# Weight sums moved forward by one slot, and three more units by seven products

## The chip, the cores and the metric

The kernel runs on one core of a Trainium2 chip. The metric is the device time of one execution in microseconds (us). The engines that matter here: TensorE (PE) multiplies, VectorE (DVE), ScalarE (ACT) and GpSimd (POOL) work elementwise, and SyncE (SP) issues nearly all DMAs. GpSimd doesn't touch the accumulators of TensorE (PSUM) in this kernel.

## The reference

Eight batches of eight heads. `x` has 512 rows of 64 numbers for each head, `state` has 32 rows. Both attend to each other, and the two readings, 544 rows for each batch, become the rows of a two-layer network with a 512 x 2048 and a 2048 x 512 matrix:

```python
a = softmax(0.125 * x @ state.T);   xread = a @ state
a2 = softmax(0.125 * state @ x.T);  sread = a2 @ x
rows = concatenate([xread, sread])        # per batch 544 rows of 8*64 = 512 numbers
h = rows @ w_in
out = (h * tanh(softplus(h))) @ w_out     # float32
```

## The kernel before

Every float32 product is made of three products of a high and a low part (high x high, high x low, low x high), each a fast matmul. The hidden width of 2048 is cut into 8 **slots** of 256. After a start in which the weights are read and batch 0 is computed, the kernel goes through **rounds** (`key`), one for each batch from 1 on. A round has 8 **lines**, one for each slot j, and the order of all work is written out by hand in `TABLE`: each word is a step, and every engine executes its instructions strictly in the order of the steps (class `InOrder`, which also is why nearly all instructions have line L73, the helper that records them).

The first layer of a line is G0 M0 G1 M1: twelve matmuls of 512 columns into two PSUM banks named `ph` (G0 the first bank, G1 the second), and ScalarE's activation out of each (`u<-ph`, M0 and M1). The pool `ps_h` has these two banks only; N0 at the end of a round, 32 small matmuls `swp` that make the next batch's first-layer weights, takes the same two banks (`first_bank`).

The second layer is done in **units** (batch, p, j): 256 of a batch's rows (p is 0 or 1) and slot j. P and p prepare a unit (`prepare`): high and low parts `gh` and `gl`. A and B consume a unit on TensorE (`consume`). At most three units are ready at once, and units are consumed some lines after they are prepared: the p=0 units of a batch in the last lines of its own round, the p=1 units in the first lines of the next round.

A unit is a 2 x 2 block product. It is done with eight block products, 12 matmuls of 512 columns (`acc_top`, `acc_end`), or in Winograd's way with seven, 21 matmuls of 256 columns into four banks (`acc_one`, `acc_two`, `acc_top`, `acc_end`). `sevens(key, p)` says for how many of a batch's eight slots the seven products are used. Seven need sums of the blocks on both sides: of the unit (`sums`, three GpSimd additions in P, then a ScalarE cast and a VectorE subtraction in p), and of the slot's weights, once for each slot. `seven_weights(j)`, the step T with the slot's number, makes the latter in four pieces, one at each mention of T in the table:

1. VectorE adds the stored high and low weights into `w_sums`; there is one buffer of it, so that this waits until the slot before is through with it.
2. GpSimd makes the four sums (VectorE for slot 7).
3. ScalarE casts them to the high parts: `wo<-w_sums` and `wx<-w_sums`. The first takes the place of a part of the slot's own weights that only eight products need.
4. VectorE subtracts for the low parts (`wo<-w_sums,wo`, `wx<-w_sums,wx`).

Where all eight slots of a (batch, p) use seven products, `merged` joins two of the last product's three matmuls into one of 512 columns, and the finish (`sums_of`, `result`) has one more addition. `sums_of` empties the banks `one` and `two` at the start of the first eight-product unit, or in the last unit.

Steps around the change: TU transposes softmax weights on VectorE (`u<-e`) and issues 16 DMAs that spread them (`e2T<-u`, on SP's queue); li issues the load of the next batch's x (`x_in`) behind them; the results' stores (`out_dram<-o`, `out_dram<-sums`) come behind these on the same queue. PR0 and PR1 transpose (`at<-e`, DVE), cast (`ah<-at`, ACT) and subtract (`al`, DVE) the other softmax; NO normalises it; X0 to X3 transpose `x_in` (DVE). sr0 and sr1 scale the state's readings (`srds`, DVE).

Of the kernel before, what the change touches and what calls it, by code (L numbers as in the profile page):

```python
# [17 lines left out]
P = 128  # L18
B, H, S, NS, D = 8, 8, 512, 32, 64
# [5 lines left out]
SLOTS = NFC // 2  # L25
# [1 line left out]
LAG = 2  # L27
WARM = 5
UNITS = 10
FIRST = 3  # L30
G = 4 * P


def as_f32(ap):
    return ap.bitcast(F32)
# [45 lines left out]
def state_attention_mish_kernel(ctx, tc, x, state, w_in, w_out, out):  # L81

    nc = tc.nc
    pe, dve, act, pool_e = (InOrder(tc, e) for e in (nc.tensor, nc.vector, nc.scalar, nc.gpsimd))
# [809 lines left out]
    S1, S3, S2, S4 = range(3, 7)  # L894
    T3, T4, T2 = range(3)
    wx = {}

    def weight_sums(j, n, m=1):


        q = 3 * j + n
        tag, first, count = ("w_in", 0, 16) if q < 16 else ("sw2", 16, 4) if q < 20 else ("x", 20, 4)
        if tag not in wx:
            wx[tag] = (const if tag == "w_in" else pool).tile([P, count, 2, 256], F32R, tag=tag, name=f"wx_{tag}", bufs=1)
        return wx[tag][:, q - first:q - first + m]

    def seven_weights(j):


        w = pool.tile([P, 4, 256], F32, tag="wt", name=f"w_sums_{j}", bufs=1)  # L910
        dve.tensor_add(
            w.rearrange("p (k e) c -> p k (e c)", k=2), as_f32(wo[j][:, :, 0]), as_f32(wo[j][:, :, 1]))
        yield
        by = dve if j == SLOTS - 1 else pool_e
        by.tensor_sub(w[:, 0], w[:, 0], w[:, 1])
        by.tensor_sub(w[:, 1], w[:, 3], w[:, 1])
        by.tensor_add(w[:, 3], w[:, 3], w[:, 0])
        by.tensor_sub(w[:, 2], w[:, 2], w[:, 3])
        yield
        cut = {5: 1, 6: 2}.get(j, 3)  # L920
        parts = [(w[:, 0], *(wo[j][:, 0, n, 256:] for n in (1, 0)))]
        for a, b in ((0, cut), (cut, 3))[:2 - cut // 3]:
            to = weight_sums(j, a, b - a)
            parts.append((w[:, 1 + a:1 + b], to[:, :, 1], to[:, :, 0]))
        for value, high, _ in parts:
            act.copy(high, value)
        yield
        for value, high, low in parts:
            dve.tensor_sub(low, value, as_f32(high))
# [34 lines left out]
    def prepare():  # L964


        unit = todo.pop(0)
        key, p, j = unit
        u = made.pop(unit).rearrange("f k h t -> f (k h) t")
        hi, lo = (  # L970
            pool.tile([P, W], F32R, tag="g", name=f"{t}_{key}_{p}_{j}", bufs=6).rearrange("f (s t) -> f s t", t=P)
            for t in ("gh", "gl"))
        parts[unit] = hi, lo
        ready.append(unit)
        if j < sevens(key, p):
            sums = pool.tile([P, 4, P], F32, tag="o", name=f"sums_{key}_{p}_{j}", bufs=2)
            pool_e.tensor_add(sums[:, :2], u[:, 1:3], u[:, 3:].to_broadcast([P, 2, P]))
            pool_e.tensor_add(sums[:, 2], sums[:, 0], u[:, 2])
            pool_e.tensor_add(sums[:, 3], sums[:, 2], u[:, 0])
            act.copy(hi[:, :3], u[:, :3])  # L980
            yield
            low_g(u[:, :3], hi[:, :3], lo[:, :3])
            act.copy(hi[:, 3:7], sums)
            low_g(sums, hi[:, 3:7], lo[:, 3:7])
        else:
            act.copy(hi[:, :4], u)
            low_g(u, hi[:, :4], lo[:, :4])
# [10 lines left out]
    def sums_of(key, p, banks):  # L998

        tag, bufs = ("g", 6) if (key, p) in ((1, 1), (B - 3, 1), (B - 2, 0)) else ("wt", 1)  # L1000
        e = banks["sums"] = pool.tile([P, 4, 256], F32, tag=tag, name=f"sums_{key}_{p}", bufs=bufs)
        one, two = (banks[n].rearrange("t (h e) -> t h e", h=2) for n in ("one", "two"))
        act.copy(e[:, 0], one[:, 0])
        dve.tensor_sub(e[:, 3], e[:, 0], one[:, 1])
        dve.tensor_add(e[:, 1:3], two, e[:, 3:].to_broadcast([P, 2, 256]))
        if sevens(key, p) < SLOTS:
            dve.tensor_add(e[:, 3], e[:, 1], two[:, 1])
        else:
            dve.scalar_tensor_tensor(e[:, 3], e[:, 1], -1.0, two[:, 1], ALU.mult, ALU.subtract)
# [63 lines left out]
    def half_slot(key, j, at):  # L1073
# [4 lines left out]
        elif ready and (ready[0][:2] != (key, 0) or ready[0][2] < j + (j == SLOTS - 1 and at)):  # L1078
# [6 lines left out]
            P G0 M0 p G1 M1  # L1085
            P G0 M0 p G1 M1 S4 S6 A S4 S4 S6 S6 T0 T0
            P G0 M0 p G1 M1 sr0 sr1 SC SC A sr0 sr1 SC MM0 MM1 w2 lx TR0 TR1 TR0 TR1
            P G0 M0 p G1 M1 T0 EE0 EE1 EX0 EX1 A T0 P p w3 B NO EE0 EE1 NO T1 T1
            P G0 M0 p G1 M1 A P p TU PR0 PR1 T1 T1 B T2
            P G0 M0 p G1 M1 PR0 PR1 P p PR0 A N0 N2 N0 N0 PR1 li P p B""",  # L1090
        2: """
            P T2 G0 M0 p G1 M1 T2 P T2 p X0 X1 A P X2 X3 p B
            P G0 M0 p G1 M1 P p S2 S2 XD A ST P p B T3
            P T3 G0 M0 p G1 M1 P p w4 A T3 P p T3 B T4
            P T4 G0 M0 p G1 M1 P p A S4 SC T4 S4 S4 SC w5 P p T4 B T5 MM0 MM1
            P G0 M0 p G1 M1 P p TR0 TR1 A P T5 TR0 TR1 p B
            P G0 M0 p G1 M1 S6 sr0 sr1 P p S6 S6 sr0 sr1 T5 EE0 EE1 EX0 EX1 A w2 w3 EE0 EE1 P p T5 B NO
            P G0 M0 p G1 M1 P p NO TU PR0 PR1 A P p B
            P G0 M0 p G1 M1 PR0 PR1 P p PR0 A N0 N2 N0 N0 PR1 li P p B""",
        3: """  # L1100
            P G0 M0 p G1 M1 P p X0 X1 A P X2 X3 T6 p B
            P T6 G0 M0 p G1 M1 P p S2 S2 XD A T6 ST T6 P p B
            P G0 M0 p G1 M1 P p w4 A P p B
            P G0 M0 p G1 M1 P p A S4 SC S4 S4 SC lx w5 P p B MM0 MM1
            P G0 M0 p G1 M1 P p TR0 TR1 A P TR0 TR1 p T7 B T7
            P G0 M0 p G1 M1 S6 sr0 sr1 P p S6 S6 sr0 sr1 EE0 EE1 EX0 EX1 A w2 w3 EE0 EE1 P p B T7 NO
            P G0 M0 p G1 M1 P p T7 NO TU PR0 PR1 A P p B""",
        "steady": """
            P G0 M0 p G1 M1 P p X0 X1 A P X2 X3 p B
            P G0 M0 p G1 M1 P p S2 S2 XD A ST P p B  # L1110
# [32 lines left out]
    for key in [*range(1, B - 1), "s", B - 1]:  # L1143
        if key == "s":
            for i, item in enumerate(items):
                j, r, k = i // 4, i // 2 % 2, i % 2
# [66 lines left out]
        for j, line in enumerate(steps_of(key)):  # L1213
            run = {
                "G": lambda k: first_k(j, k), "M": lambda k: mish_k(j, k),
                "P": lambda _: begin(), "p": lambda _: end(),
                "A": lambda _: half_slot(key, j, 0), "B": lambda _: half_slot(key, j, 1),
                "S": visit_sw,
                "N": next_sw, "T": seven_weights, "w": again, "lx": lambda _: load_natural(), "ly": lambda _: load_last(), "li": lambda _: load_next(),
                "rm": lambda _: moving, "rt": lambda _: sread_transposed(), "W": lambda i: next(items[i]), "U": lambda _: results(), "rs": lambda _: sreads_split(),  # L1220
                "z": at0["sr"], "sr": prev["sr"], "SR": own["sr"], "mm": prev["mm"], "ee": prev["ee"], "tu": prev["tu"],
                "X": own["x"], "XD": own["xd"], "ST": own["st"], "SC": own["sc"], "MM": own["mm"], "EE": own["ee"],
                "TR": own["tr"], "EX": own["ex"], "NO": own["no"], "PR": own["pr"], "TU": own["tu"],
            }
# [37 lines left out]
```

## Time and profile before

| | us |
|---|---|
| median of 3 runs (625.06 to 626.0) | 625.77 |
| the profiled execution | 625.47 |
| its span, first to last instruction | 623.7 |
| PE busy | 616.9 (99%) |
| DVE busy | 447.4 (72%) |
| ACT busy | 367.9 (59%) |
| POOL busy | 233.2 (37%) |

The trace names instructions by what they write and read, `out<-in`. A line of the timeline has the start and the duration in us, the engine, the operation, its tiles, the shape, how many like ones follow each other, and in brackets how long the engine stood idle before and what ended that. A matmul's duration is longer than its share of the stream, since matmuls are pipelined: the pace is read from start to start.

### The profile page before, as it was taken

The numbers are of one execution on the slowest core, as the hardware profiler recorded it, in microseconds if no ns is written. First come the engines' busy times: TensorE is split into PE (matmuls) and PEld (weight loads), VectorE is DVE, ScalarE is ACT, GpSimd is POOL, SyncE is SP. The second block draws the span as 40 slices with busy tenths as digits, with TensorE's granted clock in tenths as the row PEclk, the third lists the DMA queues.
The fourth block names the chain that finished last, engine by engine and source line by source line (L and its number), as shares of the span: only waits on it lengthen the run. The fifth ranks groups of instructions, "written<-read, shape, count | busy, mean of one in ns | idle before, by whom it ended". The sixth has DMA issues, their size and how long they took to land.

```text
span 623.7 us, 13822 instructions
## 1 busy us (share of the span) xinstructions
PE 616.9 (99%) x5388; PEld 534.6 (86%) x5388; DVE 447.4 (72%) x762; ACT 367.9 (59%) x762; POOL 233.2 (37%) x348
## 2 busy tenths in 40 slices
PE   8999999999999999999999999999999999999997
PEld 6777777788888898898988898889889899898997
DVE  5999976666788885969467774869386887535364
ACT  4999876466457454665447555655456766544442
POOL 0000000236366064326632573246522744443284
PEclk9999999999999999999999999999999999999999
DMA  8995922954462164534554265515355332320011
GB/s 318 413 357 149 363 77 68 296 164 125 104 210 69 35 174 117 164 106 132 141 169 136 73 155 164 171 48 163 111 172 166 106 114 91 102 68 25 11 35 35
DMA packets 71969, 88.79 MB, mean 142 GB/s; under 512 B 13792, under 2 KB 49120, under 8 KB 71904
## 3 DMA queue, kind: packets, MB, share of 16 engines
q1 hardware_dynamic: 71472, 87.71, 44.6%
q8 instruction: 43, 0.70, 0.5%
q10 hardware_dynamic: 432, 0.20, 0.1%
q14 instruction: 22, 0.18, 0.1%
HBM read 62.85 MB, written 13.11 MB: 122 GB/s over the span
## 4 chain that ended last, share of the span: by engine, by line
PE 86%; ACT 2%; DVE 1%; DMA 1%; SPq 1%; issue 1%; ACTq 0%; DVEq 0%
PE ph L73 25%; PE acc_top L73 15%; PE acc_one L73 11%; PE acc_two L73 11%; PE acc_end L73 9%; PE swp L73 4%; PE ph_s L73 4%; PE acc L73 2%; PE srp L73 1%; DMA wor<-in_moe_w_out_dram 1%; PE acc_s_one L73 1%; PE acc_s_top L73 1%; PE acc_s_two L73 1%; PE sc L73 1%; ACT wir L73 1%
## 5 line engine op out<-in xcount | busy, mean ns | idle before, releaser
L73 POOL TENSOR_TENSOR sums<-u 128x256 f32<-128x256 f32 x96 | 77.9, 812 | 192.2 <-DVE gl L73 117.0
L73 ACT ACTIVATE u<-ph 128x256 f32<-128x256 f32 x224 | 73.5, 382 | 80.0 <-PE ph L73 78.6
L73 DVE TENSOR_TENSOR gl<-u,gh 128x384 fp32r<-128x384 f32 (+1 forms) x112 | 70.2, 627 | 69.8 <-ACT gh L73 64.5
L73 POOL TENSOR_TENSOR sums<-sums,u 128x128 f32<-128x128 f32 x192 | 113.8, 593 | 15.1
L73 DVE TENSOR_TENSOR gl<-sums,gh 128x512 fp32r<-128x512 f32 x96 | 78.7, 820 | 31.0 <-ACT gh L73 31.0
L73 ACT CAST gh<-u 128x384 fp32r<-128x384 f32 (+1 forms) x112 | 59.2, 529 | 67.4 <-PE acc_end L73 47.7
L73 PE MATMUL acc_top<-wo,gh 128*128 128x256 f32 (+1 forms) x448 | 93.5, 300 | 0.0
L73 POOL TENSOR_TENSOR w_sums<-w_sums 128x256 f32<-128x256 f32 x28 | 25.3, 902 | 152.0 <-ACT gh L73 110.5
L73 ACT CAST gh<-sums 128x512 fp32r<-128x512 f32 x96 | 59.6, 621 | 29.9 <-POOL sums L73 29.8
L73 PEld LDWEIGHTS acc_top<-wo,gh 128*128 128x128 f32 x448 | 71.2, 191 | 4.5 <-issue 1.6
L73 PE MATMUL ph<-ah,swh 128*128 128x512 f32 (+1 forms) x228 | 70.6, 391 | 0.0
L73 PE MATMUL ph<-al,swh 128*128 128x512 f32 (+1 forms) x228 | 69.9, 388 | 0.2 <-DVE al L73 0.2
L73 PE MATMUL ph<-ah,swl 128*128 128x512 f32 (+1 forms) x228 | 69.9, 388 | 0.0
L73 PE MATMUL acc_top<-wo,gl 128*128 128x256 f32 (+1 forms) x224 | 66.9, 299 | 0.0
L73 PEld LDWEIGHTS ph<-al,swh 128*128 128x128 f32 x228 | 42.5, 188 | 10.0 <-DVE al L73 0.4
L73 PEld LDWEIGHTS ph<-ah,swl 128*128 128x128 f32 x228 | 42.6, 188 | 9.3
L73 DVE TENSOR_TENSOR swl<-swp,swh 128x512 fp32r<-128x512 f32 (+1 forms) x60 | 36.3, 645 | 18.6 <-ACT swh L73 18.5
L73 PEld LDWEIGHTS ph<-ah,swh 128*128 128x128 f32 x228 | 39.5, 188 | 8.3 <-issue 0.8
L73 PEld LDWEIGHTS acc_top<-wo,gl 128*128 128x128 f32 x224 | 42.7, 191 | 1.4
L73 PE MATMUL acc<-wo,gh 128*128 128x512 f32 x128 | 40.3, 395 | 0.3 <-DVE wo L73 0.3
L73 ACT CAST swh<-swp 128x512 fp32r<-128x512 f32 (+1 forms) x60 | 30.5, 563 | 16.8 <-PE swp L73 16.8
L73 PE MATMUL acc_one<-wo,gh 128*128 128x256 f32 x192 | 39.8, 289 | 0.0
(233 smaller groups left out, 1393.6 us busy)
## 6 DMA issues: line engine op xcount, KB each, us to landing
w_in<-w_in_again SPq DMA_DIRECT2D x27, 1024.0 KB, 6.1
x<-in_x_dram SPq DMA_DIRECT2D x32, 256.0 KB, 4.4
wir<-in_moe_w_in_dram SPq DMA_DIRECT2D x16, 512.0 KB, 9.4
wor<-in_moe_w_out_dram SPq DMA_DIRECT2D x16, 512.0 KB, 8.9
x_rows<-x_turned SPq DMA_DIRECT2D x56, 128.0 KB, 2.4
out_dram<-sums SPq DMA_DIRECT2D x25, 256.0 KB, 4.4
x_in<-in_x_dram SPq DMA_DIRECT2D x24, 256.0 KB, 4.2
w_in_again<-w_in_sb SPq DMA_DIRECT2D x4, 1024.0 KB, 7.1
```

Of the source, the lines that this page charges most:

```text
L73: made = method(*args, **kwargs)
```

## The change

Slot 1's weight sums (T1) move from the end of line 5 and the line after to stand directly behind slot 0's in line 5 of round 1. Each later slot's steps move up: T3 takes T2's places, T4 takes T3's, and so on, and T2 comes into line 6 of round 1, where T1 ended before, with all four pieces in that line. With sums ready one slot earlier, `FIRST` goes from 3 to 4 and `sevens` gives 7 for (2, 0) and 8 for (2, 1): the units (1, 1, 3), (2, 0, 6) and (2, 1, 7) are made by seven products, and the eight units of (2, 1) by merged ones. Slot 7's four sums move from VectorE to GpSimd.

```diff
--- before.py
+++ after.py
@@ -27,7 +27,7 @@
 LAG = 2
 WARM = 5
 UNITS = 10
-FIRST = 3
+FIRST = 4
 G = 4 * P
 
 
@@ -911,7 +911,7 @@
         dve.tensor_add(
             w.rearrange("p (k e) c -> p k (e c)", k=2), as_f32(wo[j][:, :, 0]), as_f32(wo[j][:, :, 1]))
         yield
-        by = dve if j == SLOTS - 1 else pool_e
+        by = pool_e
         by.tensor_sub(w[:, 0], w[:, 0], w[:, 1])
         by.tensor_sub(w[:, 1], w[:, 3], w[:, 1])
         by.tensor_add(w[:, 3], w[:, 3], w[:, 0])
@@ -950,7 +950,7 @@
         todo += [(key, p, j) for p in range(1 if key == "s" else 2) for j in range(SLOTS)]
 
     def sevens(key, p):
-        return {(1, 0): 0, (1, 1): FIRST, (2, 0): SLOTS - 2, (2, 1): SLOTS - 1}.get((key, p), SLOTS)
+        return {(1, 0): 0, (1, 1): FIRST, (2, 0): SLOTS - 1}.get((key, p), SLOTS)
 
     def merged(key, p):
 
@@ -1085,26 +1085,26 @@
             P G0 M0 p G1 M1
             P G0 M0 p G1 M1 S4 S6 A S4 S4 S6 S6 T0 T0
             P G0 M0 p G1 M1 sr0 sr1 SC SC A sr0 sr1 SC MM0 MM1 w2 lx TR0 TR1 TR0 TR1
-            P G0 M0 p G1 M1 T0 EE0 EE1 EX0 EX1 A T0 P p w3 B NO EE0 EE1 NO T1 T1
-            P G0 M0 p G1 M1 A P p TU PR0 PR1 T1 T1 B T2
+            P G0 M0 p G1 M1 T0 EE0 EE1 EX0 EX1 A T0 T1 T1 P p w3 B NO EE0 EE1 NO
+            P G0 M0 p G1 M1 T1 A T1 P p TU T2 T2 PR0 PR1 T2 T2 B T3
             P G0 M0 p G1 M1 PR0 PR1 P p PR0 A N0 N2 N0 N0 PR1 li P p B""",
         2: """
-            P T2 G0 M0 p G1 M1 T2 P T2 p X0 X1 A P X2 X3 p B
-            P G0 M0 p G1 M1 P p S2 S2 XD A ST P p B T3
-            P T3 G0 M0 p G1 M1 P p w4 A T3 P p T3 B T4
-            P T4 G0 M0 p G1 M1 P p A S4 SC T4 S4 S4 SC w5 P p T4 B T5 MM0 MM1
-            P G0 M0 p G1 M1 P p TR0 TR1 A P T5 TR0 TR1 p B
-            P G0 M0 p G1 M1 S6 sr0 sr1 P p S6 S6 sr0 sr1 T5 EE0 EE1 EX0 EX1 A w2 w3 EE0 EE1 P p T5 B NO
-            P G0 M0 p G1 M1 P p NO TU PR0 PR1 A P p B
+            P T3 G0 M0 p G1 M1 T3 P T3 p X0 X1 A P X2 X3 p B
+            P G0 M0 p G1 M1 P p S2 S2 XD A ST P p B T4
+            P T4 G0 M0 p G1 M1 P p w4 A T4 P p T4 B T5
+            P T5 G0 M0 p G1 M1 P p A S4 SC T5 S4 S4 SC w5 P p T5 B MM0 MM1
+            P G0 M0 p G1 M1 P p TR0 TR1 A P TR0 TR1 p B
+            P G0 M0 p G1 M1 S6 sr0 sr1 P p S6 S6 sr0 sr1 T6 T6 EE0 EE1 EX0 EX1 A w2 w3 EE0 EE1 P p T6 B NO
+            P G0 M0 p G1 M1 T6 P p NO TU PR0 PR1 A P p B
             P G0 M0 p G1 M1 PR0 PR1 P p PR0 A N0 N2 N0 N0 PR1 li P p B""",
         3: """
-            P G0 M0 p G1 M1 P p X0 X1 A P X2 X3 T6 p B
-            P T6 G0 M0 p G1 M1 P p S2 S2 XD A T6 ST T6 P p B
+            P G0 M0 p G1 M1 P p X0 X1 A P X2 X3 T7 p B
+            P T7 G0 M0 p G1 M1 P p S2 S2 XD A T7 ST T7 P p B
             P G0 M0 p G1 M1 P p w4 A P p B
             P G0 M0 p G1 M1 P p A S4 SC S4 S4 SC lx w5 P p B MM0 MM1
-            P G0 M0 p G1 M1 P p TR0 TR1 A P TR0 TR1 p T7 B T7
-            P G0 M0 p G1 M1 S6 sr0 sr1 P p S6 S6 sr0 sr1 EE0 EE1 EX0 EX1 A w2 w3 EE0 EE1 P p B T7 NO
-            P G0 M0 p G1 M1 P p T7 NO TU PR0 PR1 A P p B""",
+            P G0 M0 p G1 M1 P p TR0 TR1 A P TR0 TR1 p B
+            P G0 M0 p G1 M1 S6 sr0 sr1 P p S6 S6 sr0 sr1 EE0 EE1 EX0 EX1 A w2 w3 EE0 EE1 P p B NO
+            P G0 M0 p G1 M1 P p NO TU PR0 PR1 A P p B""",
         "steady": """
             P G0 M0 p G1 M1 P p X0 X1 A P X2 X3 p B
             P G0 M0 p G1 M1 P p S2 S2 XD A ST P p B

```

## Rows read from the trace of the kernel before

**Rows 1.** The page: busy time by engine, its share, instructions.
```profile
PE 616.9 (99%) x5388; PEld 534.6 (86%) x5388; DVE 447.4 (72%) x762; ACT 367.9 (59%) x762; POOL 233.2 (37%) x348
```

**Rows 2.** Waits of PE between 70 and 330 us: total, times, longest.
```profile
PE acc L73 <- DVE wo L73: 0.3, 1, 0.3
```

**Rows 3.** Timeline of PE: starts of (1,1,0), (1,1,1), (1,1,4), (1,1,5).
```profile
148.54 0.40 PE L73 MATMUL acc_one<-wo,gh 128*128 128x256 f32 x2
...
151.05 0.40 PE L73 MATMUL acc_one<-wo,gh 128*128 128x256 f32 x2
...
164.32 0.61 PE L73 MATMUL acc_top<-wo,gh 128*128 128x512 f32 x2
...
167.04 0.61 PE L73 MATMUL acc_top<-wo,gh 128*128 128x512 f32 x2
```

**Rows 4.** Timeline of DVE, lines 5 and 6 of round 1.
```profile
128.52 0.69 DVE L73 TENSOR_TENSOR gl<-u,gh 128x512 fp32r<-128x512 f32 x1 [3.43 <-ACT gh L73]
...
132.79 1.22 DVE L73 TENSOR_TENSOR w_sums<-wo 128x1024 f32<-128x1024 f32 x1
...
134.53 1.30 DVE L73 STREAM_TRANSPOSE u<-e 128x512 f32<-128x512 f32 x2
...
138.82 1.16 DVE L73 TENSOR_TENSOR wx_w_in<-w_sums,wx_w_in 128x768 fp32r<-128x768 f32 x1 [1.50 <-ACT wx_w_in L73]
```

**Rows 5.** Timeline of POOL: T1's four sums.
```profile
134.16 3.76 POOL L73 TENSOR_TENSOR w_sums<-w_sums 128x256 f32<-128x256 f32 x4 [18.67 <-DVE w_sums L73]
```

**Rows 6.** Operations on `w_sums`: count, shortest/median/longest of one in ns.
```profile
L73 POOL TENSOR_TENSOR w_sums<-w_sums x28: 727/924/1294, 111.9 to 230.0; 128x256 f32<-128x256 f32 x28
```

**Rows 7.** Timeline of ACT, lines 6 and 7 of round 1.
```profile
137.95 0.83 ACT L73 CAST wx_w_in<-w_sums 128x768 fp32r<-128x768 f32 x1 [2.30 <-POOL w_sums L73]
138.69 1.20 ACT L73 ACTIVATE u<-ph 128x256 f32<-128x256 f32 x4
...
140.79 0.65 ACT L73 CAST gh<-u 128x512 fp32r<-128x512 f32 x1
```

**Rows 8.** Timeline of PE, end of round 1.
```profile
141.03 1.96 PE L73 MATMUL swp<-w_in,bd 64*32 64x256 f32 x64
```

**Rows 9.** Timeline of DVE, line 5 of round 2 to line 0 of round 3.
```profile
196.20 0.46 DVE L73 TENSOR_SCALAR srds<-srp,rs 128x64 f32<-128x64 f32 x2
...
199.53 0.69 DVE L73 TENSOR_TENSOR gl<-sums,gh 128x512 fp32r<-128x512 f32 x1
200.14 0.42 DVE L73 TENSOR_TENSOR wo<-w_sums,wo 128x256 fp32r<-128x256 f32 x1
...
202.22 0.67 DVE L73 TENSOR_REDUCE s<-e 128x16 f32<-128x512 f32 x1
...
205.99 1.30 DVE L73 STREAM_TRANSPOSE u<-e 128x512 f32<-128x512 f32 x2
...
225.47 1.22 DVE L73 TENSOR_TENSOR w_sums<-wo 128x1024 f32<-128x1024 f32 x1 [0.75 <-DMA out_dram<-sums]
...
227.08 1.23 DVE L73 TENSOR_TENSOR gl<-sums,gh 128x512 fp32r<-128x512 f32 x1
```

**Rows 10.** Timeline of POOL: one unit's three sums.
```profile
195.90 0.75 POOL L73 TENSOR_TENSOR sums<-u 128x256 f32<-128x256 f32 x1
196.73 1.01 POOL L73 TENSOR_TENSOR sums<-sums,u 128x128 f32<-128x128 f32 x2
```

**Rows 11.** Timeline of SP's DMA queue, from line 7 of round 2.
```profile
207.36 10.09 SPq L403 DMA_DIRECT2D e2T<-u  x16
...
219.71 1.39 SPq L693 DMA_DIRECT2D out_dram<-sums  x2
```

**Rows 12.** Timeline of PE: unit (2,1,3), first matmul with its sums' low part.
```profile
229.60 0.28 PE L73 MATMUL acc_one<-wx_w_in,gl 128*128 128x256 f32 x1
```

**Rows 13.** Timeline of PE in the first microseconds.
```profile
1.36 2.50 PE L73 MATMUL warm<-ident 128*128 128x128 f32 x10 [1.36 <-POOL ident masks.py:199]
...
6.13 1.07 PE L73 MATMUL st<-ident,sn 128*64 128x128 f32 x8
```

## The prediction

> **What bounds the kernel now.** I read the page first: TensorE is busy for 616.9 of 623.7 us, no other engine for more than 72% [rows 1]. A matmul's duration holds pipelining, so 99% alone doesn't say that the stream is dense; the waits do. Between 70 and 330 us, the stretch in which every edit lies, TensorE waited once, 0.3 us, for the weights of batch 0 [rows 2]. From then on nothing that the other engines do is late for it. So two things count: how many columns the stream loses, and whether an edit uses up the slack of something that TensorE now finds ready. Gains on VectorE, ScalarE or GpSimd are worth nothing, and no stall is there to remove.
>
> **What the seven products save.** An eight-product unit takes 167.04 - 164.32 = 2.72 us from start to start, a seven-product unit 151.05 - 148.54 = 2.51 [rows 3]: 0.21 each, 0.63 for three. The paces are 2.72/12 = 0.227 us for 512 columns and 2.51/21 = 0.120 for 256, so a merged last product takes 0.227 + 0.120 = 0.347 in place of 0.359: 0.012 for each of the eight units of (2,1), 0.1 in all. Together **-0.7 us**. This is all that the change can bring. Its price off TensorE, for each of the three units: three sums on GpSimd, another cast and another subtraction; for the merged finish one addition. In rounds 4 and on every unit pays this without a wait of TensorE, so I cost them at nothing where no weight sums are made beside them. Slot 7's sums on GpSimd take VectorE out of work at a place where nothing waits: nothing.
>
> **The move of T1 and T2 in round 1.** T1's addition now lies in a hole: VectorE idled 3.43 us before 128.52 [rows 4], and GpSimd had nothing. Free. At 132.79, where it stood, T1's two subtractions come instead (0.42 [rows 9] and 0.96 to 1.16 [rows 4]); that is an exchange of 1.2 against some 1.3, and TU starts at about 134.6 instead of 134.53. T2's addition must wait for the one buffer of `w_sums`, and stands behind TU, whose two transposes take 1.3: it starts at 135.85 and ends at 137.1. GpSimd begins 0.15 after the end of an addition (T1: 134.01, then 134.16 [rows 5]), so T2's sums begin at 137.2. T1's took 3.76 [rows 5]; the 28 sums have 0.727, 0.924 and 1.294 as their least, median and longest [rows 6], so four take 2.9 to 5.2. T2's run beside two transposes and one subtraction only; I take 3.5, near the median, and they end at 140.75.
>
> The Trainium skill, in "SBUF — State Buffer", section "Who interferes with whom", says that VectorE and GpSimd share one pair of ports, that only a VectorE instruction with two inputs in SBUF (or in a two-port mode) contends with GpSimd's reads, and that the second one then blocks for the whole instruction. By that, transposes would cost T2's sums nothing; they would take about 3.1, the stall below would be 1.3, and the sum 0.4 lower. T1's four were of 0.74 to 1.06 us with both kinds beside them, which doesn't decide it.
>
> Now what is queued behind. T2's large cast (`wx<-w_sums`) stands in line 6 and waits for all four sums. ScalarE executes in order, so the four activations of line 7 (M0, M1) stand behind it, and the casts of PR0, PR1 and of unit (1,0,7). In the kernel before this very thing happens with T1: the cast waited 2.30 us for GpSimd and began at 137.95, and the activations ended at 138.69 + 1.20 = 139.89 [rows 7]. That was in time, because N0, which needs both `ph` banks emptied by them, came at 141.03 [rows 8]. With the cast at 140.78 instead of 137.95 all this is 2.8 late: the activations end at 142.7, and N0, with the two banks of the pool taken, starts at 142.75: TensorE stands for **1.7 us**. The cast of (1,0,7), ending at 141.44 before [rows 7], ends at 144.3; N0's 1.9 us last until 144.65, so it is no second wait; its low part, behind T3's addition on VectorE, may be late by 0.1. I take **+1.8**; the ends are 1.1 (sums of 2.9) and 3.4 (sums of 5.2). Nothing later gives this back, as TensorE has no idle time to fill. T3's steps stand where T2's stood, and its weights are needed one unit later; unit (1,1,3)'s new subtractions have a few tenths to spare. T4 and T5 take places of T3 and T4. I count nothing for these.
>
> **The move of T6 into line 5 of round 2.** Times here are those of the kernel before; all of them shift with the first stall. T5's addition of 1.2 us has left the end of line 3, so that VectorE, busy without a break from there, ends `srds` not at 196.66 [rows 9] but at about 195.1 (0.3 of it an estimate for subtractions with no GpSimd beside them). T6's addition follows, until 196.3, and its four sums on GpSimd until 199.95. But the three sums of unit (2,0,5) are now behind them on GpSimd, 1.84 us [rows 10], until 201.8; then the cast, 0.62, and the subtraction `gl<-sums`, which began at 199.53 [rows 9], begins at 202.4 and ends at 203.1. NO's second part, at 202.22 before, with T5's subtractions (2.08 us, 200.14 to 202.22 [rows 9]) ahead of it, starts 0.85 late although these are gone. In line 6 T6's subtractions (1.4, as GpSimd is idle then; 2.08 at most) and the second subtraction of (2,0,6), 0.6, stand ahead of TU, which was at 205.99 [rows 9]: TU is 2.85 late.
>
> TU is the head of a chain on SP's queue: 16 issues of 10.09 us, the load of x, the store of (2,0) at 219.71 [rows 11]. The slot's addition in line 0 of round 3 waits for that store (225.47, idle 0.75 [rows 9]), since `sums` of (2,0) and `w_sums` are one buffer; behind it on VectorE stands `gl<-sums` of unit (2,1,3), which ended at 227.08 + 1.23 = 228.31 [rows 9]. TensorE wanted it at 229.60 [rows 12]: a slack of 1.29. The chain has none before that, so 2.85 late leaves a stall of **1.55**. Its ends: nothing, if TU is less than 1.3 late (T6's sums quick, VectorE ahead), and 3.2, if T6's sums take 5.2.
>
> **The sum.** -0.7 + 1.8 + 1.5 = +2.6 us. The profiled execution of 625.47 (a span of 623.7 and 1.77 around it) becomes 628.1; it lies 0.3 under the median of the runs, so the forecast for the median is 628.4.
>
> **The rivals.**
>
> *No stall, the other side.* GpSimd's sums of T2 are done before ScalarE is needed, and TensorE finds all its banks empty: 625.77 - 0.7 = 625.1. It decides at N0: the large cast must begin before 141.03 - 1.97 = 139.05 (1.97 from its start to the end of the activations [rows 7]), so T2's addition 1.7 us earlier than I place it, or all four sums in 1.8 us. For it: in the kernel before TensorE waited for nothing here, so much slack is about. Against: the buffer of `w_sums` and the order of VectorE, which put the addition behind TU; and no sum was shorter than 0.727 [rows 6].
>
> *The first stall alone.* VectorE keeps more of its lead in lines 4 and 5 of round 2, or the chain on SP is shorter, and the 1.29 us hold: 625.77 - 0.7 + 1.8 = 626.9. For it: the second stall is a difference of long chains. Against: three things of 0.6 to 1.4 us come in ahead of TU.
>
> *The delay piles up.* T6's sums are slow, and unit (2,0,5) and the activations of line 6, behind its cast on ScalarE, are late for TensorE too, another 1.5: 629.9. For it: GpSimd's spread of 0.727 to 1.294.
>
> *The clock falls.* In the first microseconds the 128-column matmuls went at 0.25 us each (2.50 for ten), from 6.13 on at 0.134 [rows 13]: half rate for up to 4.8 us, a loss of 2.4. If a stall of 1.8 us brought that back, once, the time would be 630.8. The Trainium skill ("TensorE: Matmul & The Clock Gate", "HAM oscillation — how this bites in real kernels") says that TensorE's clock falls to half after idling for long enough in one piece. No row here has so long a gap after the start, which leaves it open; the granted clock of the trace is at full speed, 2.4 GHz.
>
> **How the numbers follow.** Forecast 0.45, its own range 627.4 to 629.4 (sums between 2.9 and 4.3 us); first stall alone 0.22; no stall 0.20; pile-up 0.08; clock 0.05. What a measurement can tell from no change is about 0.2%, 1.25 us: 624.5 to 627.0. No case reaches under 624.5 by its rows; I leave 0.04 for a gain that I don't see. Within lie the rest of "no stall" and over half of "first stall alone", 0.16 + 0.14 = 0.30; slower is 0.66. The range of 625.0 to 630.3 goes from the whole saving without a stall to the pile-up.
>
> **What would show it.** In the profile after: T2's four sums on GpSimd right behind TU, beginning near 137.2; ScalarE waiting for them until 140.5 or later; a wait of TensorE for ScalarE's `u` ahead of `swp` at the end of round 1, 1 to 2.5 us; `e2T<-u` of round 2 issued over 1.3 us later than TensorE's own shift; a wait of TensorE for VectorE's `gl` in unit (2,1,3). The chain that ended last would then pass through GpSimd in these two places. The units (1,1,3), (2,0,6) and (2,1,7) would take 2.51 us each from start to start. The prediction is wrong if `swp` follows unit (1,0,6) at once, and wrong in its second part if TU isn't late or if VectorE has the low part of (2,1,3) before TensorE asks for it.

## The result, and the profile after

The changed kernel takes 631.5 us (median of 5 runs, 630.81 to 632.71); beside it the kernel before took 625.51 (624.87 to 626.0). The ratio is 1.010, interval 1.0089 to 1.0111: 6 us slower, and above the range of 625.0 to 630.3. The profiled execution took 631.46, its span is 629.7 (before: 623.7).

The page answers [rows 1]: TensorE is busy 1.9 us longer over a span that is 6.0 longer.

```profile
PE 618.8 (98%) x5407; PEld 535.8 (85%) x5407; DVE 449.0 (71%) x762; ACT 369.8 (59%) x765; POOL 240.3 (38%) x361
```

TensorE's waits between 70 and 330 us answer [rows 2] (total, times, longest):

```profile
PE acc_one L73 <- DVE gl L73: 2.5, 2, 2.1
PE swp L73 <- ACT u L73: 1.1, 1, 1.1
PE acc_top L73 <- ACT gh L73: 0.2, 1, 0.2
```

The first two are the two forecast stalls, at the forecast places. To see what each cost, I set TensorE's starts of the same matmuls in the two traces side by side. The changed kernel was 0.45 ahead at 136 us; 0.42 of that was there at 115 us, before its first moved instruction (T1's addition, 124.85). Such an offset of the start lies between -1.1 and +2.0 us in the traces below. From 136 us on it loses:

| stretch, time of before | lost | what |
|---|---|---|
| 136 to 154 | +2.29 | first stall |
| 154 to 170 | -0.23 | (1,1,3) by seven |
| 170 to 224 | +0.33 | (2,0,6) by seven, -0.21; (2,0,7) late, +0.54 |
| 224 to 232 | +4.27 | second stall, unit (2,1,3) |
| 232 to 250 | -0.22 | (2,1,7) by seven, merged products |
| sum | +6.44 | |

Behind 250 the two run in step to the end; 6.44 less the 0.45 of the start is the 6.0 by which the span grew.

**The saving came.** Timeline of TensorE, unit (1,1,3) and the next product, against [rows 3]:

```profile
160.67 0.40 PE L73 MATMUL acc_one<-wo,gh 128*128 128x256 f32 x2
...
163.19 0.40 PE L73 MATMUL ph<-ah,swh 128*128 128x512 f32 x1
```

2.52 us from start to start; 2.72 by eight products. The three units and the merged products gave 0.23 + 0.21 + 0.22 = 0.66.

**The first stall.** Timelines of GpSimd, ScalarE and TensorE at the end of round 1:

```profile
137.08 3.25 POOL L73 TENSOR_TENSOR w_sums<-w_sums 128x256 f32<-128x256 f32 x4 [7.34 <-DVE w_sums L73]
```
```profile
140.36 0.83 ACT L73 CAST wx_w_in<-w_sums 128x768 fp32r<-128x768 f32 x1 [2.11 <-POOL w_sums L73]
141.10 1.20 ACT L73 ACTIVATE u<-ph 128x256 f32<-128x256 f32 x4
```
```profile
141.81 2.50 PE L73 MATMUL swp<-w_in,bd 64*32 64x256 f32 x64 [1.15 <-ACT u L73]
```

T2's sums are made in 3.25 us; the large cast waits for them, the four activations stand behind the cast, and `swp` begins when the first bank is free and then takes 2.50 in place of 1.96 [rows 8] because the second is emptied last (it is 64 matmuls in both traces, not the 32 named above). So 1.2 is lost ahead of `swp`, 0.5 in it, and 0.5 by the units behind it.

**The second stall.** First SP's queue and VectorE, against [rows 9, 11]:

```profile
212.45 10.61 SPq L403 DMA_DIRECT2D e2T<-u  x16
223.16 2.06 SPq L136 DMA_DIRECT2D x_in<-in_x_dram  x4
225.32 0.92 SPq L693 DMA_DIRECT2D out_dram<-sums  x2
```
```profile
226.04 1.38 DVE L73 STREAM_TRANSPOSE x_turned<-x_in 128x512 f32<-128x512 f32 x2 [1.72 <-DMA x_in<-in_x_dram]
229.45 1.46 DVE L73 STREAM_TRANSPOSE x_turned<-x_in 128x512 f32<-128x512 f32 x2 [2.03 <-DMA x_in<-in_x_dram]
231.66 1.23 DVE L73 TENSOR_TENSOR w_sums<-wo 128x1024 f32<-128x1024 f32 x1 [0.75 <-DMA out_dram<-sums]
232.80 0.55 DVE L73 TENSOR_TENSOR gl<-u,gh 128x384 fp32r<-128x384 f32 x1
233.27 1.22 DVE L73 TENSOR_TENSOR gl<-sums,gh 128x512 fp32r<-128x512 f32 x1
```

Then TensorE, against [rows 12]:

```profile
230.95 0.40 PE L73 MATMUL acc_one<-wo,gh 128*128 128x256 f32 x2
233.40 0.39 PE L73 MATMUL acc_one<-wo,gl 128*128 128x256 f32 x1 [2.05 <-DVE gl L73]
...
234.54 0.58 PE L73 MATMUL acc_one<-wx_w_in,gl 128*128 128x256 f32 x1 [0.46 <-DVE gl L73]
...
237.73 0.63 PE L73 MATMUL ph<-ah,swh 128*128 128x512 f32 x2
```

Shifted by the 1.94 of delay that TensorE had by then, `acc_one<-wx_w_in,gl` was due at 229.60 + 1.94 = 231.54 and came at 234.54: 3.00 late. From it to the end of the unit 3.19 us passed, against 231.52 - 229.60 = 1.92 before: 1.27 more, in which TensorE waits for nothing. That is the clock. Windows of 1 us (the column after those of the five engines is the granted clock):

```profile
233.00:234.00 1.00, 0.60 (x3) 0.42 (x3) 1.00 (x2) 0.03 (x1) 0.94 (x1) 0.91 0.85 206
234.00:235.00 1.00, 0.54 (x3) 0.46 (x3) 1.00 (x2) 0.38 (x1) 0.98 (x1) 0.50 0.83 201
235.00:236.00 1.00, 1.00 (x7) 1.00 (x7) 1.00 (x2) 0.00 (x0) 0.92 (x2) 0.50 0.86 207
236.00:237.00 1.00, 1.00 (x6) 1.00 (x6) 1.00 (x2) 0.00 (x0) 0.92 (x2) 0.50 0.81 198
237.00:238.00 1.00, 1.00 (x8) 0.91 (x7) 1.00 (x3) 0.75 (x2) 0.93 (x2) 0.88 0.45 101
```

At 233.8, 0.4 us behind the first wait and ahead of the second, the clock went to 0.50, which is 1.2 GHz, through three whole windows and parts of two more. The mean clock of the run is 0.997, and it is 0.996 or 0.997 in all five runs of this kernel.

### The profile page after: what moved, and what is told of

Read it like the earlier page. It is cut to its first block, busy times and chain, and to the rows that moved or that the text cites. A ratio compares the mean times of both kernels' runs of the same rounds, so it can differ in the third digit from the quotient of the medians.

```text
span 629.7 us, 13880 instructions
## 1 busy us (share of the span) xinstructions
PE 618.8 (98%) x5407; PEld 535.8 (85%) x5407; DVE 449.0 (71%) x762; ACT 369.8 (59%) x765; POOL 240.3 (38%) x361
## 4 chain that ended last, share of the span: by engine, by line
PE 70%; DVE 7%; SPq 5%; DMA 3%; ACT 3%; issue 2%; POOL 2%; DVEq 0%; ACTq 0%; POOLq 0%
PE ph L73 19%; PE acc_top L73 11%; PE acc_one L73 11%; PE acc_two L73 10%; PE acc_end L73 6%; PE ph_s L73 4%; PE swp L73 4%; SPq L403 3%; DVE gl L73 2%; DMA w_in_again<-w_in_sb 1%; PE acc L73 1%; PE srp L73 1%; POOL w_sums L73 1%; PE acc_s_one L73 1%; PE acc_s_top L73 1%
## 5 line engine op out<-in xcount | busy, mean ns | idle before, releaser
L73 POOL TENSOR_TENSOR sums<-u 128x256 f32<-128x256 f32 x99 | 80.6, 814 | 186.6 <-DVE gl L73 114.6
L73 POOL TENSOR_TENSOR sums<-sums,u 128x128 f32<-128x128 f32 x198 | 116.4, 588 | 15.5
L73 DVE TENSOR_TENSOR gl<-u,gh 128x384 fp32r<-128x384 f32 (+1 forms) x112 | 71.5, 638 | 65.9 <-ACT gh L73 63.9
L73 POOL TENSOR_TENSOR w_sums<-w_sums 128x256 f32<-128x256 f32 x32 | 27.3, 852 | 155.9 <-ACT gh L73 110.2
L73 ACT CAST gh<-sums 128x512 fp32r<-128x512 f32 x99 | 61.5, 621 | 38.3 <-POOL sums L73 38.1
L73 PE MATMUL acc_one<-wo,gh 128*128 128x256 f32 x198 | 41.1, 290 | 0.0
L73 PE MATMUL acc_two<-wo,gh 128*128 128x256 f32 x198 | 40.1, 284 | 0.0
```

Source lines behind the costliest of these rows:

```text
L73: made = method(*args, **kwargs)
```

## The experiments

Unless its text says otherwise, each version is the changed kernel with the edit shown. Its ratio is against the kernel before, measured again beside it (medians of 625.12 to 625.28). Because the start differs between executions, the traces are compared by what TensorE loses from 136 us on, in the stretches of the table above. A row shows the one profiled execution, the median all runs; where the clock fell in some runs only, the two need not agree:

| | 136-154 | 154-170 | 170-224 | 224-232 | 232-250 | sum | median, us |
|---|---|---|---|---|---|---|---|
| changed kernel | +2.29 | -0.23 | +0.33 | +4.27 | -0.22 | +6.44 | 631.5 |
| t2_casts_later | 0 | +1.45 | +0.32 | +4.00 | -0.19 | +5.58 | 631.7 |
| t6_in_t5_places | +1.86 | -0.23 | -0.26 | +1.72 | +0.08 | +3.17 | 627.82 |
| both_moves | 0 | +0.89 | -0.27 | +1.06 | +0.08 | +1.76 | 627.5 |
| t7_other_buffer | +1.82 | -0.23 | +0.31 | +1.81 | +0.09 | +3.80 | 629.67 |
| three_moves | 0 | +1.05 | -0.27 | +0.01 | -0.21 | +0.58 | 626.46 |
| t2_between_p | +0.06 | +0.32 | -0.27 | +0.01 | 0 | +0.12 | 625.19 |
| t3_behind | +0.16 | +1.20 | -0.24 | 0 | +0.05 | +1.17 | 625.95 |
| t7_vector_best | 0 | +0.87 | -0.24 | +0.01 | +1.48 | +2.11 | 627.26 |
| moves_alone | +2.25 | -0.03 | 0 | +3.38 | +0.38 | +5.99 | 629.14 |

**t2_casts_later: T2's casts and subtractions leave line 6.**

```
-  ... P p TU T2 T2 PR0 PR1 T2 T2 B T3
-  P G0 M0 p G1 M1 PR0 PR1 P p PR0 A N0 N2 N0 N0 PR1 li P p B
+  ... P p TU T2 T2 PR0 PR1 B
+  P G0 M0 p G1 M1 PR0 PR1 P p PR0 A N0 N2 N0 N0 PR1 li P T2 p T2 B T3
```

> Only T2's casts and subtractions are moved, from line 6 of round 1 to the end of line 7; T3's addition stands behind them as before. Theory (ScalarE stands before T2's large cast until GpSimd is through, and M0, M1 of line 7, which empty the two banks that N0 needs, stand behind it): the 2.3 us that the changed kernel is behind at unit (1,1,0) go, the second stall stays as it is, since its chain moves along with TensorE: 631.5 - 2.3 = 629.2. Rival (GpSimd and VectorE are simply full there, whatever the order): the wait ahead of swp or of (1,0,7) stays within 0.5 us, 631.0 to 631.5.

631.7 (629.92 to 633.03), ratio 1.0098 [1.0076, 1.012]. The median didn't fall to the 629.2 expected (the one run of four in which the clock stayed at 1.0 took 629.92), but the first stall is gone: TensorE's delay doesn't change from 136 to 154 us. ScalarE's order was its cause. The gain was given back two units later: with T2's casts late, T3's addition and sums come later too, and GpSimd has the sums of (1,1,2) and (1,1,3) late, +1.45.

**t6_in_t5_places: T6 goes back to where T5 stood.**

```
-  ... P p T5 B MM0 MM1
-  P G0 M0 p G1 M1 P p TR0 TR1 A P TR0 TR1 p B
-  P G0 M0 p G1 M1 S6 sr0 sr1 P p S6 S6 sr0 sr1 T6 T6 EE0 ...
-  P G0 M0 p G1 M1 T6 P p NO TU PR0 PR1 A P p B
+  ... P p T5 B T6 MM0 MM1
+  P G0 M0 p G1 M1 P p TR0 TR1 A P T6 TR0 TR1 p B
+  P G0 M0 p G1 M1 S6 sr0 sr1 P p S6 S6 sr0 sr1 T6 EE0 ...
+  P G0 M0 p G1 M1 P p NO TU PR0 PR1 A P p B
```

> Only T6 is moved back, into the places that T5 had in the kernel before (end of line 3, lines 4 and 5 of round 2); everything else is the changed kernel, seven products in (2,0,6) included. Theory (T6's sums ahead of unit (2,0,5)'s on GpSimd and its subtractions ahead of TU make the chain TU, e2T, x_in, store late): TU comes about 2.5 us earlier against TensorE, unit (2,1,3) doesn't wait or waits under 0.5 us, TensorE's clock doesn't fall: 631.5 - 4.3 - 0.4 = 626.8. Rival (slot 7's sums on GpSimd instead of VectorE slow the subtraction of (2,1,3)): nothing of this changes, 631.5.

627.82 (627.17 to 628.68), ratio 1.004 [1.0027, 1.0053]. The second stall falls from 4.27 to 1.72 and the mean clock is 0.999 or 1.0 in all five runs. The time is a microsecond above the 626.8 expected: TensorE still waits 0.68 and 0.52 at (2,1,3). So T6's place is the larger part of the second stall, and not all of it.

**both_moves: the two edits above together, and nothing else.**

> Both edits together, with the three units by seven products and the merged products kept. Theory: no wait of TensorE is left between 130 and 250 us, and what remains is the saving of 0.7 us: 624.8 against 625.5 of the kernel before, ratio 0.999. Rival (the additional sums of three units cost TensorE something too): 625.5 or more.

627.5 (627.02 to 628.17), ratio 1.0037 [1.0022, 1.0051]: over two us more than expected. T2's casts and T6 are out of the way and 1.76 us remain, at a place that the prediction didn't have and at (2,1,3) again. Round 2, line 0, timeline of GpSimd: T3's sums ahead of those of (1,1,2) and (1,1,3).

```profile
149.00 3.75 POOL L73 TENSOR_TENSOR w_sums<-w_sums 128x256 f32<-128x256 f32 x4 [4.10 <-DVE w_sums L73]
152.71 0.74 POOL L73 TENSOR_TENSOR sums<-u 128x256 f32<-128x256 f32 x1
153.53 1.60 POOL L73 TENSOR_TENSOR sums<-sums,u 128x128 f32<-128x128 f32 x2
```

And round 3, line 0, timeline of VectorE: T7's addition still waits for the store of (2,0), ahead of the subtractions of (2,1,3).

```profile
228.04 1.23 DVE L73 TENSOR_TENSOR w_sums<-wo 128x1024 f32<-128x1024 f32 x1 [0.80 <-DMA out_dram<-sums]
229.18 0.55 DVE L73 TENSOR_TENSOR gl<-u,gh 128x384 fp32r<-128x384 f32 x1
229.65 1.22 DVE L73 TENSOR_TENSOR gl<-sums,gh 128x512 fp32r<-128x512 f32 x1
```

TU began here at 207.91, 1.92 later than before and 1.3 later than TensorE's own delay of 0.63, with T6's subtractions out of its way: (2,0,6) by seven products does that, as its two subtractions hold VectorE for 1.89 there (205.13 to 207.02), where the one of an eight-product unit held it for 0.60.

**t7_other_buffer: slot 7's `w_sums` in a buffer of its own.**

```
-  w = pool.tile([P, 4, 256], F32, tag="wt", ...
+  w = pool.tile([P, 4, 256], F32, tag="sc" if j == SLOTS - 1 else "wt", ...
```

> The changed kernel with w_sums of slot 7 in a buffer of its own (that of the scores, unused at that time), so that its addition in line 0 of round 3 no longer waits for the store of (2,0). Theory: the two transposes ahead of it on VectorE wait for x_in of the same late chain, so only the last 0.75 us of the wait go: 2.95 us of waits in (2,1,3) become 2.2, and the time 630.8, or 629.2 if TensorE's clock then doesn't fall. Rival (the buffer shared with the results' sums is the cause): the whole stall goes, 627.2.

629.67 (628.13 to 631.97), ratio 1.0071 [1.0046, 1.0095]. Without the wait for the store the unit loses 1.81, not 4.27; 1.27 of that difference is the clock, which stayed at 1.0 in this profiled run, and the lateness alone fell from 3.00 to 1.7. The transposes X0 and X2 still wait for x (1.91 and 1.50), which TU's lateness delays in the same way. So the shared buffer is one of two paths from TU to TensorE. In two of its four runs the mean clock was 0.997, in two 1.0: spans of 628.7 and 630.2 against 626.3 and 627.0.

**three_moves: T7's addition behind the subtractions of (2,1,3)**, added to both_moves.

```
-  P G0 M0 p G1 M1 P p X0 X1 A P X2 X3 T7 p B
+  P G0 M0 p G1 M1 P p X0 X1 A P X2 X3 p T7 B
```

> T2's casts behind N0, T6 in T5's places, and T7's addition in line 0 of round 3 behind the two subtractions of unit (2,1,3) in place of ahead of them. Theory: what was left of the second stall with the first two edits (1.04 us at unit (2,1,3)) is T7's addition, which waited 0.80 for the store of (2,0) and took 1.23 ahead of these subtractions; behind them it costs nothing, and the two waits of about half a microsecond at units (1,1,2) and (1,1,3) stay. Time 627.5 - 1.0 = 626.5. Rival: the subtractions are late because the batch's x is late (the four transposes of x_in stand ahead of them too, and waited for its load); then 0.5 or more of the wait stays, and the time is 627.0 to 627.5.

626.46 (625.29 to 628.72), ratio 1.0022 [1.001, 1.0033]. As the theory had it: +0.01 at (2,1,3), although X0 to X3 still wait for x. What was late there was the addition.

**t2_between_p: T2 ahead of and within N0, p ahead of X2 and X3**, added to three_moves.

```
-  P G0 M0 p G1 M1 PR0 PR1 P p PR0 A N0 N2 N0 N0 PR1 li P T2 p T2 B T3
+  P G0 M0 p G1 M1 PR0 PR1 P p T2 PR0 A N0 N2 N0 T2 N0 PR1 T3 li P p B
-  P T3 G0 M0 p G1 M1 T3 P T3 p X0 X1 A P X2 X3 p B
+  P T3 G0 M0 p G1 M1 T3 P T3 p X0 X1 A P p X2 X3 B
```

> As three_moves, but T2's casts stand between the preparation of (1,0,7) and N0, its subtractions within N0, T3's addition within line 7 in place of its end, and in line 0 of round 2 the second half of unit (1,1,3)'s preparation stands ahead of the transposes X2 and X3. Theory: with T2's casts at the end of line 7, T3's sums on GpSimd came in ahead of the sums of units (1,1,2) and (1,1,3), which made TensorE wait for their low parts, 0.9 us in two; with T3's sums earlier and the subtractions ahead of two transposes these waits are gone. The saving of 0.73 shows: 625.1 - 0.7 + 0.5 at most = 624.4 to 624.9. Rival: the casts of T2 wait for GpSimd ahead of N0's own cast and of (1,0,7)'s, and a wait of up to 1 us comes back at the end of round 1: 625.5 to 626.5.

625.19 (624.11 to 627.34, 12 runs), beside 625.24 of the kernel before; ratio 0.9999 [0.9989, 1.001]. Both stalls are gone and no wait of the first stall came back, yet the saving doesn't show: over (1,1,2) and (1,1,3) TensorE loses 0.32 where it should gain 0.23 (it loses 0.55 at (1,1,2), whose sums stand behind T3's on GpSimd), and 0.2 more at (2,1,5), whose sums stand behind T7's. The best version equals the kernel before.

**t3_behind: T3's sums behind those of (1,1,2)**, in place of ahead of them.

```
-  P T3 G0 M0 p G1 M1 T3 P T3 p X0 X1 A P p X2 X3 B
+  P G0 M0 p G1 M1 P T3 p X0 X1 A T3 P T3 p X2 X3 B
```

> As t2_between_p, but in line 0 of round 2 T3's four sums on GpSimd stand behind the sums of unit (1,1,2) in place of ahead of them, its casts and subtractions behind X0 and X1. Theory: the half microsecond that TensorE still waited for the low part of (1,1,2) came from T3's sums (4.2 us on GpSimd, 147.9 to 152.1) ahead of this unit's; now it is gone and nothing else is late, since T3's weights are needed one unit later. Time 625.2 - 0.5 = 624.7, which is the saving of 0.7 with 0.2 of it lost. Rival: T3's casts now wait on ScalarE behind which the activations of line 1 stand, or (1,1,3)'s sums come late behind T3's; then a wait of 0.5 to 1 us comes in at (1,1,3) or at the next ph, and the time is 625.2 to 626.0.

625.95 (624.91 to 627.0, 11 runs), ratio 1.0009 [0.9998, 1.0019]. The rival was right. T3's cast now waits on ScalarE for T3's sums, and the casts of (1,1,2) and (1,1,3) stand behind it:

```profile
153.75 0.84 ACT L73 CAST wx_w_in<-w_sums 128x768 fp32r<-128x768 f32 x1 [2.04 <-POOL w_sums L73]
154.49 0.51 ACT L73 CAST gh<-u 128x384 fp32r<-128x384 f32 x1
155.52 0.62 ACT L73 CAST gh<-sums 128x512 fp32r<-128x512 f32 x1 [0.52 <-POOL sums L73]
```

It is the first stall's mechanism once more. T3 must be done one unit earlier than before, and around it GpSimd and ScalarE have no room of 0.5 us in the two orders tried.

**t7_vector_best: slot 7's sums on VectorE as before**, in t3_behind.

```
-  by = pool_e
+  by = dve if j == SLOTS - 1 else pool_e
```

> As t3_behind, with slot 7's four sums on VectorE as in the kernel before. Theory (of the prediction: this part of the change costs and brings nothing): the same as t3_behind within 0.3. Rival 1: VectorE's sums, four more operations in line 1 of round 3, make a subtraction of (2,1,4) late: 0.5 to 1.5 longer. Rival 2: T7's sums on GpSimd stand ahead of the sums of (2,1,4) and cost TensorE the 0.17 us seen there; then 0.2 shorter.

627.26 (626.39 to 630.18), ratio 1.0031 [1.0017, 1.0046]: 1.3 slower than t3_behind, the first rival in size, though at another place, and the second rival's unit is (2,1,5). The four sums take 2.50 on VectorE ahead of `swl`, and the next layer waits. Timelines of VectorE and TensorE:

```profile
229.87 2.50 DVE L73 TENSOR_TENSOR w_sums<-w_sums 128x256 f32<-128x256 f32 x4
...
233.36 1.28 DVE L73 TENSOR_TENSOR swl<-swp,swh 128x512 fp32r<-128x512 f32 x2
```
```profile
234.09 1.10 PE L73 MATMUL ph<-ah,swl 128*128 128x512 f32 x2 [1.05 <-DVE swl L73]
```

Here slot 7's sums belong on GpSimd: where T7 now stands, that part of the change is worth over a microsecond, not nothing.

**moves_alone: the changed kernel's order with the units of before.**

```
-  FIRST = 4
+  FIRST = 3
-  ... (2, 0): SLOTS - 1}
+  ... (2, 0): SLOTS - 2, (2, 1): SLOTS - 1}
```

The three units, by eight products, then read weights of which T has replaced a part: that changes their values, not the number or the shapes of the matmuls.

> The changed kernel's order of T1 to T7 with the number of seven-product units as before: (1,1,3), (2,0,6) and (2,1,7) by eight products, no merged products in (2,1). Theory: both stalls come from the places of T2 and T6 alone; TU still waits behind T6's subtractions. The first stall is as in the changed kernel (1.1 of waiting for u, 2.3 in all); the second keeps over 2.5 us of delay, and only the saving of 0.7 is missing: 631.0 to 632.5. Rival: the three sums of (2,0,6) and its second subtraction ahead of TU are a large part of the second stall; without them TU is 1 to 1.5 earlier, the wait at (2,1,3) is 1 to 1.5, the clock stays at full speed, and the time is 628.5 to 630.

629.14 (627.8 to 631.07), ratio 1.0062 [1.0042, 1.0081]: the rival's range in the median. In the profiled run, the slowest, the clock still fell (0.997); in the other three it was 0.999 to 1.0. The first stall is there as it was (waits of 1.1). From the timeline of TensorE:

```profile
233.60 0.39 PE L73 MATMUL acc_one<-wx_w_in,gl 128*128 128x256 f32 x1 [0.52 <-DVE gl L73]
```

TU begins at 209.58 instead of 211.08, which is 1.75 earlier against TensorE. Of this 0.9 arrives: the low part of (2,1,3) is 2.14 late instead of 3.00, mainly because the four loads of x took 3.06 to issue in place of 2.06. Unit (2,1,3) takes 5.62 (230.86 to 236.48) instead of 6.78. So the sums of (2,0,6) are a part of the second stall, 0.9 of the 3.0 us of lateness, and without them the clock stayed up in three of four runs.

**before_three_adds, before_four_adds, before_five_adds: a delay of known size in the kernel before**, slot 6's addition made three, four and five times (the edit shows four).

```
-  dve.tensor_add(w..., wo..., wo...)
+  for _ in range(4 if j == 6 else 1):
+      dve.tensor_add(w..., wo..., wo...)
```

> The kernel before with slot 6's addition three times: 2 x 1.22 = 2.44 us more on VectorE. With the slack of 1.29 TensorE waits 1.15 to 1.4 at unit (2,1,3). Theory of the clock: a wait of this length leaves it at full speed, mean granted clock 1.0 in every run; time 625.2 + 1.4 = 626.6. Rival: the clock falls at shorter waits too in some runs; then some runs show 0.997 and 1.1 to 1.4 us more, 628.

> The kernel before, with slot 6's addition done four times in place of once (the same result each time): 3 x 1.22 = 3.66 us more on VectorE in line 0 of round 3 and nothing else. Theory: the slack of unit (2,1,3)'s low part is 1.29, so TensorE waits 2.4 in one or two pieces, and a wait of this length brings the clock to half for a stretch of 3.4 us, which costs another 1.3 to 1.7: 625.1 + 3.7 to 4.1 = 628.8 to 629.2. Rival: the clock fell in the changed kernel for another reason (the first stall and the waits before it add up); then the granted clock stays at 1.0 and the time is 627.5.

> The kernel before with slot 6's addition five times: 4 x 1.22 = 4.88 us more. TensorE waits 3.6 at unit (2,1,3). Theory: the clock falls in every run (0.997), costing 1.1 to 1.4 beside the wait: 625.2 + 3.6 + 0.6 (later waits, as with four) + 1.3 = 630.7. Rival: the fall hangs on something other than the length of the wait, and some runs keep 1.0, at 629.4.

| additions | added on VectorE | lost to the end of (2,1,3) in the profiled run | its clock | runs with clock 0.997 | median |
|---|---|---|---|---|---|
| 3 | 2.44 | 1.22 | 0.999 | 1 of 8 | 626.98 |
| 4 | 3.66 | 2.76 | 1.0 | 3 of 4 | 629.61 |
| 5 | 4.88 | 4.63 | 0.997 | 4 of 4 | 630.54 |

The ratios are 1.0028 [1.0018, 1.0038], 1.0068 [1.0053, 1.0084] and 1.0082 [1.0066, 1.0099]. The 0.999 is a stretch at half clock behind the last matmul (from 624.2 us), not in this unit. The first row gives a slack of 2.44 - 1.22 = 1.22, close to the 1.29 read from [rows 9, 12]; the second, 3.66 - 2.76 = 0.90, which stays open. With four additions the spans were 626.6 without a fall and 627.7 to 628.0 with one, a difference that the spread of the start could make by itself. The traces give the price better: from the last wait of this unit until 250 us TensorE loses 0.4 with three and with four additions, where the clock stayed up, and 1.6 with five. With five, the clock fell in the profiled run in the same way as in the changed kernel (windows as above):

```profile
234.00:235.00 1.00, 1.00 (x8) 1.00 (x7) 1.00 (x2) 0.00 (x0) 0.92 (x2) 0.63 0.97 250
235.00:236.00 1.00, 1.00 (x6) 1.00 (x6) 1.00 (x3) 0.12 (x1) 1.00 (x2) 0.50 0.98 358
236.00:237.00 1.00, 1.00 (x4) 0.81 (x3) 1.00 (x3) 1.00 (x3) 0.92 (x2) 0.50 0.65 252
```

So a delay of this unit brings the fall in the kernel before as well; the first stall isn't needed for it.

## Why the prediction was wrong

**The saving of 0.7: right.** 0.66 measured.

**The first stall of 1.8: right in mechanism, 0.5 short.** T2's sums took 3.25, in place of 3.5, and the cast began at 140.36 + 0.45 = 140.8 in time of before, as forecast (140.78). That is luck in part, as the sums began 0.3 later than forecast (137.08 + 0.45) and took 0.25 less. The wait ahead of `swp` and its slower run make 1.76, the forecast 1.7. But the casts, subtractions and sums behind the activations came late as well, to unit (1,0,7) and line 0 of round 2: 0.5 where I had 0.1. The Trainium skill, in "SBUF — State Buffer", section "Who interferes with whom", has transposes leave GpSimd alone; three of T2's four sums took 0.74, those beside VectorE's transposes among them, and 3.25 lies nearer to the 3.1 that I had worked out by that rule than to my 3.5. It didn't help, as the delay behind the cast was larger than the difference.

**The second stall of 1.5: this is the step that failed.** Place and wait were as forecast; the size was 4.27. The prediction left out a wait of VectorE for ScalarE ahead of TU, took the chain behind TU at its old length, and its sum had the clock at full speed.

*TU was later than 2.85, and its chain longer.* The prediction counted only VectorE's queue ahead of TU: NO's second part 0.85 late, T6's three subtractions, 1.4, and "the second subtraction of (2,0,6), 0.6". NO's second part was not late: it began at 203.66, 0.17 earlier than in [rows 9] against TensorE. T6's subtractions took 1.82 (205.94 to 207.76), the first subtraction of (2,0,6) 0.21 more than that of an eight-product unit, and the second one stood for 1.01, because its sums weren't there. That wait is the missing term, and its path runs over ScalarE. Its timeline in the kernel before, and then in the changed one:

```profile
198.88 0.62 ACT L73 CAST gh<-sums 128x512 fp32r<-128x512 f32 x1
199.51 1.28 ACT L73 ACT_TABLE_LOAD   x1
200.81 1.21 ACT L73 ACTIVATE u<-ph 128x256 f32<-128x256 f32 x4
```
```profile
202.40 0.62 ACT L73 CAST gh<-sums 128x512 fp32r<-128x512 f32 x1 [3.59 <-POOL sums L73]
202.93 0.40 ACT L73 CAST wo<-w_sums 128x256 fp32r<-128x256 f32 x1
203.24 0.61 ACT L73 CAST wx_sw<-w_sums 128x512 fp32r<-128x512 f32 x1
203.76 0.40 ACT L73 CAST wx_x<-w_sums 128x256 fp32r<-128x256 f32 x1
204.18 1.28 ACT L73 ACT_TABLE_LOAD   x1
205.47 1.22 ACT L73 ACTIVATE u<-ph 128x256 f32<-128x256 f32 x4
```

The cast of (2,0,5) waits for GpSimd, which has T6's sums first; T6's three casts (1.25) and the table load stand behind it, then the activations of line 6, 4.66 later than before where TensorE was 1.61 late. From them GpSimd makes the sums of (2,0,6), and VectorE, ahead of TU, waits:

```profile
206.48 1.08 POOL L73 TENSOR_TENSOR sums<-u 128x256 f32<-128x256 f32 x1 [4.11 <-ACT u L73]
```
```profile
203.66 0.68 DVE L73 TENSOR_REDUCE s<-e 128x16 f32<-128x512 f32 x1
...
205.94 0.42 DVE L73 TENSOR_TENSOR wo<-w_sums,wo 128x256 fp32r<-128x256 f32 x1
...
207.76 0.81 DVE L73 TENSOR_TENSOR gl<-u,gh 128x384 fp32r<-128x384 f32 x1
209.58 0.69 DVE L73 TENSOR_TENSOR gl<-sums,gh 128x512 fp32r<-128x512 f32 x1 [1.01 <-ACT gh L73]
...
211.08 1.30 DVE L73 STREAM_TRANSPOSE u<-e 128x512 f32<-128x512 f32 x2
```

TU is 5.09 later than in [rows 9], 3.48 later than TensorE (-0.17 + 1.82 + 0.21 + 1.01 + 0.61). Behind it the 16 issues took 0.52 longer and the store landed 0.58 later after its issue; less the 0.33 that TensorE lost meanwhile, T7's addition is 4.25 late. With the slack of 1.29 that leaves 2.96, and 3.00 were measured. Against the forecast of 1.55 these are -1.02 at NO, +0.42 at T6's subtractions, +1.23 at (2,0,6), +0.77 in the chain. The prediction had named ScalarE's waiting cast only in the rival "the delay piles up" (0.08, 629.9), and there as a wait of TensorE; here it fed the same stall. In line 6 itself TensorE didn't wait for it.

*The clock rival happened.* It had a chance of 0.05, and it goes together with the forecast and doesn't stand beside it: a longer second stall is what brings it. It cost 1.27 in the profiled run, not the 2.4 that I took from the start; there I had compared matmuls of two shapes (`128*128` and `128*64`), in a stretch for which the profile's windows show the granted clock at 1.00, so that price was not well founded. The first stall, a wait of 1.15, brought no fall.

The account: -0.66 + 2.29 + 3.00 + 1.27 + 0.54 = 6.44. The 0.54 is unit (2,0,7): its cast stood on ScalarE behind the casts of PR0 and PR1, which waited 2.14 for the transposes behind TU; with TU earlier, in t6_in_t5_places, it is gone. The forecast had -0.7 + 1.8 + 1.5. The ends of the prediction's own terms, -0.7 + 3.4 + 3.2, would have reached 631.7, above the 630.3 that it stated; they would have been right by luck, as they asked for sums of 5.2 us, and T2's took 3.25, T6's 3.40.

**The other edits.** T1's move was free, as costed: TensorE's lead is the same at 115 and at 136 us within 0.03. Slot 7's sums on GpSimd show no loss in the changed kernel: from 232 to 250 us it gains 0.22, the forecast 0.3 (0.21 for a unit, 0.1 for the merged products); no run there has them on VectorE. "I count nothing" for T3 was right only as long as the first stall gave it time: without that stall the earlier T3 costs 0.3 to 1.5 us at (1,1,2) and (1,1,3), saving of (1,1,3) included, which is where most of the saving goes in the best version. Two slips of the working change nothing: the time from the large cast to the end of the activations is 1.94 by [rows 7], not 1.97, and [rows 4] show 1.16 for the large subtraction, not a range from 0.96.

## What to carry to other kernels

Where every engine executes in order, follow a moved step through all of its engines, and then through what stands behind it on each: here the instruction that mattered was an activation of another unit, behind a cast that waited for sums. Read the slack from the trace, but expect the stall to be more than lateness less slack once it is some microseconds: TensorE's clock may fall on top. A saving of a tenth of a per cent by needing a result earlier is worth trying only after finding the room for it on all engines that make it.

## What the runs showed of the hardware that wasn't expected

- TensorE's clock went to 1.2 GHz behind a wait of 2.05 us, ahead of one of 0.46, in the profiled run of the changed kernel; by the mean clock it fell in all five. With four additions (waits of 1.7 and 0.5 in the profiled run) it fell in three of four runs, with three (0.7 in two waits) in one of eight; in moves_alone (1.2 and 0.5) in one of four, in t7_other_buffer (0.8 and 0.5) in two of four, in t6_in_t5_places (0.7 and 0.5) in none of five. So the same program may or may not lose some 1.2 us. With five additions TensorE had been multiplying for 1.1 us since its last wait (233.16) when the clock fell (234.26). Why it falls in one run and not in the next stays open. The Trainium skill ("TensorE: Matmul & The Clock Gate", "HAM oscillation — how this bites in real kernels") ties the fall to a gap in one piece; the runs agree that on the whole longer waits bring it more often, and moves_alone (a fall at 234.5) and five additions show it behind two waits with matmuls between them.
- The subtraction `gl<-sums` of unit (2,1,3), 128x512, took 1.22 us beside GpSimd's weight sums (233.27 in the changed kernel) and 0.68 with GpSimd idle (228.02 in t7_vector_best). Four sums of 128x256 took 2.50 on VectorE and 3.2 to 4.3 on GpSimd.
